# Seven-product quads whose sums are accumulated by TensorE on a copied bank, with a new plan of the work

## The chip, the cores and the metric

The kernel runs on one core of a Trainium2 chip. The metric is the device time of one execution in microseconds (us). PE is TensorE, DVE is VectorE, ACT is ScalarE, POOL is GpSimd, SP is SyncE. PE writes its products to PSUM, eight banks of 128 x 512 fp32, here the tiles bank0 to bank7; every engine but POOL works on them in this kernel.

## What is computed

Three parts follow each other: an attention, an expert with an ELU, and an expert with a gated SiLU behind an RMS norm.

```python
q_n, k_n = rmsnorm(q, g_q), rmsnorm(k, g_k)            # (4, 12, 448, 64)
scores = scale * np.matmul(q_n, k_n.transpose(0, 1, 3, 2))
attn = softmax(scores)                                  # row maximum taken off
x = np.matmul(attn, v).transpose(0, 2, 1, 3).reshape(1792, 768)

h = x @ w_in                                            # 768 -> 2048
g = np.where(h > 0, h, np.exp(np.minimum(h, 0)) - 1)
x = g @ w_out                                           # 2048 -> 768

xn = x / np.sqrt(np.mean(x * x, -1, keepdims=True) + 1e-6) * rms_g
g = xn @ w_gate                                         # 768 -> 1536
out = (g / (1 + np.exp(-g)) * (xn @ w_val)) @ w_out     # 1536 -> 768
```

The accuracy of fp32 is kept: each operand of a product is split into a rounded high part and the rest, and a product takes three matmuls (high by high, high by low, low by high).

## The kernel before

**Tiles.** Activations lie transposed, 128 features by the 448 tokens of one batch, so a matmul is 128 x 128 weights by 128 x 448 activations. `mm3` (L1329) issues the three matmuls of one split pair, as one step. `product` (L1343) sums several of them into a bank for the plain products.

**Stages.** `STAGES` (L718) has five: the first expert for batch 0, for batch 1, the second expert for batches 0 and 1, the first for 2 and 3, the second for 2 and 3. The attention is woven into the first ones. By `PLAIN` (L719) the first two stages and one group of the third use plain products; everything after that, from about 590 us on, is made of quads.

**Quads.** Two batches and two halves of the features make 2 x 2 blocks, and `quad` (L1363) forms the product of two such block matrices with seven block products in place of eight (Strassen's scheme in Winograd's form): `A11`, `A12`, `A22` are weight blocks and `S1` to `S4` sums of weight blocks, made beforehand; `B11`, `B21`, `B22` are activation blocks and `T1` to `T4` sums of them, which `combo` (L1390) makes. `part` (L1349) takes the next bank of the ring `r_m` and sums the two or three blocks of one product into it. There are 40 quads: 20 for gate and value of the second expert (`gv_quad`, ten calls of two, three blocks a product), 8 for the hidden layer of the first (`h_quad`, three blocks) and 12 for outputs (two blocks). The first product is copied to SBUF, and DVE adds up the others:

```python
copy(p1, part(w["A11"], tx["B11"]), "va")
p6 = part(w["S2"], tx["T2"]); tt(u2, p6, p1, ALU.add)
p2 = part(w["A12"], tx["B21"]); tt(p2, p2, p1, ALU.add); eat(0, 0, p2)
p7 = part(w["S3"], tx["T3"]); tt(u3, p7, u2, ALU.add)
```

`eat` is what uses a finished block (an activation function, a product with the gate, an addition to the output). `USE` (L753) is the order in which the weight blocks of a quad are loaded and taken in the last stage.

**Weights.** Raw weights come from HBM (`wr<-wst`, SP's queue), are split into high and low parts (`wc`, `wt`, `w`, `p`) by DVE, ACT and POOL while they are first used, and parts of them are stored to HBM (`pair<-w`, `kept<-wc`). In the last stage ready blocks are loaded by `b_ahead` (L806), which issues `w<-pair` on POOL's queue.

**The order of the work.** Nothing is issued directly. Every step is added to a `Plan` (L36) with its price on each engine that may run it; `tt`, `copy` and the like name the engines ("vag" is DVE, ACT or POOL), and a step with a PSUM operand can't go to POOL. `schedule` (L150) then lists the steps: `PASSES` forward and backward rounds from a random start (`SEED`), and after them the `MOVES`, each of which shakes the ranks of the steps planned between two times, and lists anew. `forward` (L216) takes the next step of the engine that is free first; where a step has a choice, the engine's own end plus a constant, `WAIT`, is compared with that of the others (L290). The constants are 2.5 for DVE, 0.3 for ACT and 0.4 for POOL. `issue` (L330) emits the steps in that order, so each engine runs its own in order, and fills empty places of PE before the first product with warm-up matmuls on the tile `small` (`IDLE`). All instructions are recorded at one line, L445, so tiles tell them apart. `phase` (L701) deals out the banks: three for `r_m` during the attention, six from phase 2, eight at the end.

## Time and profile before

| | us |
|---|---|
| timed runs | 1213.25, 1214.23, 1218.28 (median 1214.23) |
| profiled execution, first to last instruction (its span) | 1212.0 |
| PE busy | 1196.5 (99%) |
| DVE busy | 932.9 (77%) |
| ACT busy | 715.4 (59%) |
| POOL busy | 824.7 (68%) |

The page gives no time of its own for the profiled execution but its span; the timed runs lie above it. The engines work side by side, so their busy times don't add up to the span. In the rows further down, `out<-in` are tiles without their numbers, `xN` is how many instructions a row holds, and `[0.68 <-DVE pj]` says that the engine stood idle for 0.68 us and that DVE's step on the tile pj ended that.

### The profile page before, as it was taken

To read this page: it belongs to the slowest core of one execution; us is meant where nothing else is said; L and a number is where in the kernel's file an instruction comes from. 1 tells how busy PE (TensorE), PEld (TensorE's weight loads), DVE (VectorE), ACT (ScalarE), POOL (GpSimd) and SP (SyncE) were. 2 spreads that over 40 slices of the span, in tenths; PEclk is the share of its full clock that TensorE was granted. 3 is DMA by queue.
4 is the path that set the end of the run, shared out by engine and by line. 5 is a ranking of instruction groups with operands and counts; after the bars stand their busy time and mean duration, and the time that the engine had idled before them with its cause. 6 is when DMAs were issued, how large, how long until landed. Compare 5 with 4: busy or idle time off the path is not lost.

```text
span 1212.0 us, 18931 instructions
## 1 busy us (share of the span) xinstructions
PE 1196.5 (99%) x6262; PEld 1005.5 (83%) x6262; DVE 932.9 (77%) x1559; ACT 715.4 (59%) x1482; POOL 824.7 (68%) x686
## 2 busy tenths in 40 slices
PE   8999999999999999999999999999999999999998
PEld 7558777778777777777998999999999989999997
DVE  8788999889654579653498799957975799478687
ACT  6987878768666577655564465757653753222121
POOL 3678778788555485545887789857974878265362
PEclk9999999999999999999999999999999999999999
DMA  7678877878545598855499899696794855766766
GB/s 255 224 240 271 284 263 252 256 227 297 156 136 178 178 318 291 271 172 184 168 312 350 280 343 326 187 285 196 244 354 162 265 200 174 243 210 202 239 200 204
DMA packets 128294, 290.71 MB, mean 240 GB/s; under 512 B 16190, under 2 KB 77380, under 8 KB 128196
## 3 DMA queue, kind: packets, MB, share of 16 engines
q1 hardware_dynamic: 107028, 221.52, 53.7%
q0 software_dynamic: 12528, 58.99, 15.4%
q10 hardware_dynamic: 8640, 8.99, 2.9%
q8 instruction: 49, 0.80, 0.3%
q14 instruction: 49, 0.40, 0.1%
HBM read 193.34 MB, written 96.11 MB: 239 GB/s over the span
## 4 chain that ended last, share of the span: by engine, by line
PE 87%; DVE 5%; ACT 4%; issue 2%; DMA 1%; POOL 0%; ACTq 0%; DVEq 0%; POOLq 0%
PE bank L445 87%; DVE bank L445 1%; ACT tbig L445 1%; DMA w<-pair 1%; DVE wc L445 1%; ACT p L445 1%; DVE ss L445 1%; DVE late L445 1%; DMA pair<-late 1%; DVE last L445 0%; ACT pt L445 0%; DVE tbig L445 0%; DVE xs L445 0%; DMA tk<-tok 0%; DVE wt L445 0%
## 5 line engine op out<-in xcount | busy, mean ns | idle before, releaser
L445 PE MATMUL bank<-xs,w 128*128 128x448 f32 x1755 | 405.4, 370 | 0.8 <-ACT tbig L445 0.8
L445 PE MATMUL bank<-gbig,w 128*128 128x448 f32 x1675 | 377.3, 370 | 0.4 <-DMA w<-pair 0.4
L445 PEld LDWEIGHTS bank<-xs,w 128*128 128x128 f32 x1755 | 322.7, 188 | 33.1 <-issue 5.9
L445 PEld LDWEIGHTS bank<-gbig,w 128*128 128x128 f32 x1675 | 309.1, 188 | 32.6 <-issue 6.1
L445 POOL TENSOR_TENSOR w<-wc,w 128x768 fp32r<-128x768 f32 (+1 forms) x100 | 184.4, 1845 | 62.0 <-ACT w L445 57.8
L445 PE MATMUL bank<-late,w 128*128 128x448 f32 x740 | 185.8, 366 | 0.1
L445 DVE TENSOR_REDUCE bank<-bank 128x1 f32<-128x448 f32 x168 | 99.3, 624 | 65.2 <-PE bank L445 64.7
L445 PEld LDWEIGHTS bank<-late,w 128*128 128x128 f32 x740 | 138.8, 188 | 12.0 <-DVE late L445 0.4
L445 ACT ACTIVATE pt<-bank 128x384 f32<-128x384 f32 (+2 forms) x191 | 85.4, 459 | 43.5 <-PE bank L445 34.9
L445 ACT ACTIVATE p<-bank,nm,rr 128x448 f32<-128x448 f32 x126 | 90.0, 718 | 25.7 <-DVE nm L445 12.9
L445 DVE SCALAR_TENSOR_TENSOR wc<-wc,wt 128x768 int32<-128x768 int32 x68 | 92.4, 1360 | 14.5 <-ACT wc L445 8.7
L445 ACT ACTIVATE w<-wc 128x768 fp32r<-128x768 f32 (+1 forms) x80 | 62.6, 786 | 38.8 <-PE bank L445 33.2
L445 DVE TENSOR_TENSOR tbig<-bank,tbig 128x448 f32<-128x448 f32 x101 | 61.5, 618 | 18.1 <-PE bank L445 15.6
L445 DVE TENSOR_SCALAR wt<-wr 128x768 uint16<-128x768 uint16 x68 | 73.4, 1080 | 2.1 <-DMA wr<-wst 1.9
L445 POOL TENSOR_TENSOR w<-p,w 128x768 fp32r<-128x768 f32 (+1 forms) x33 | 62.1, 1886 | 18.5 <-ACT w L445 18.2
L445 PE MATMUL bank<-ident,p 128*128 128x128 f32 x441 | 71.2, 276 | 2.2 <-ACT pt L445 1.5
L445 POOL DMA_DIRECT2D w<-pair x60 | 33.5, 558 | 55.5 <-PE bank L445 54.4
L445 PEld LDWEIGHTS bank<-ident,p 128*128 128x128 f32 x441 | 53.5, 140 | 19.5 <-ACT pt L445 5.6
L445 ACT ACTIVATE tbig<-bank 128x448 f32<-128x448 f32 x69 | 37.1, 540 | 53.1 <-PE bank L445 45.9
L445 POOL TENSOR_SCALAR w<-wc 128x768 fp32r<-128x768 f32 (+1 forms) x39 | 33.3, 854 | 48.7 <-PE bank L445 45.6
L445 ACT ACTIVATE wt<-wr 128x768 uint16<-128x768 uint8 x46 | 50.1, 1088 | 11.8 <-DVE wc L445 10.6
L445 POOL TENSOR_TENSOR ql<-rw,qh 128x512 fp32r<-128x512 f32 x32 | 45.9, 1442 | 15.3 <-ACT qh L445 14.4
(247 smaller groups left out, 2199.5 us busy)
## 6 DMA issues: line engine op xcount, KB each, us to landing
wr<-wst SPq DMA_DIRECT2D x68, 768.0 KB
pair<-w SPq DMA_DIRECT2D x68, 384.0 KB
w<-pair POOLq DMA_DIRECT2D x33, 768.0 KB, 4.9
kept<-wc SPq DMA_DIRECT2D x52, 384.0 KB
wc<-kept SPq DMA_DIRECT2D x48, 384.0 KB
w<-pair POOLq DMA_DIRECT2D x24, 512.0 KB, 4.6
rw<-qk SPq DMA_DIRECT2D x21, 512.0 KB
tk<-tok SPq DMA_DIRECT2D x20, 480.0 KB
```

The source lines that it names most:

```text
L445: return lambda *a, **k: f(*[real(x) for x in a], **{n: real(x) for n, x in k.items()})
```

## The change

`quad` no longer copies the first product to SBUF. The product stays in its bank, a copy of it goes to a second bank `u`, and later products are accumulated by PE onto one or the other: `S2`, `S3` and `A22` onto `u`, `A12` onto the first product, `S4` onto that of `S1`. What `u` held after `S2` and after `S3` is copied to SBUF (`s2`, `s3`), and two additions remain. `part` gets the bank to add to, `mm3` and `block` pass that on, `USE` follows the new order, `combo` turns the sign of `T4`, and `phase` deals `r_m` its banks in another order. `Plan` gets other constants: more passes, another seed, `WAIT` of 0.6 for DVE (it was 2.5) and 1.2 for POOL (it was 0.4), 143 moves in place of 20, and a seventh number in a move which, where it is not negative, replaces POOL's constant for the time window of the move (in steps of 25 us).

```diff
-    PASSES = 11
-    SEED = 47
+    PASSES = 20
+    SEED = 12
     MOVES = (
-        (645977, 260.9, 275.9, 8.0, 1, 0),
...
+        (456330, 559.5, 659.5, 0.0, 1, 1, 3.0),
+        (918116, 941.4, 961.4, 8.0, 1, 0, -1.0),
...
-    WAIT = {"v": 2.5, "a": 0.3, "g": 0.4}
+    WAIT = {"v": 0.6, "a": 0.3, "g": 1.2}
...
+        self.bias = [self.WAIT["g"]] * 80
...
-        for seed, lo, hi, size, own, more in self.MOVES:
+        for seed, lo, hi, size, own, more, bias in self.MOVES:
+            if bias >= 0:
+                for k in range(len(self.bias)):
+                    if lo <= 25 * k < hi:
+                        self.bias[k] = bias
...
-                mine = t + alts[e][0] + self.WAIT[e]
-                other = min(max(free[o], t) + self.BACK * back[o] + alts[o][0] + self.WAIT[o] for o in alts if o != e)
+                wait = dict(self.WAIT, g=self.bias[min(79, int(t / 25))])
+                mine = t + alts[e][0] + wait[e]
+                other = min(max(free[o], t) + self.BACK * back[o] + alts[o][0] + wait[o] for o in alts if o != e)
...
-    def block(mms, price):
+    def block(mms, price, onto=False):
...
-                T.matmul(o, l, r, start=start, stop=stop)
+                T.matmul(o, l, r, start=start, stop=stop, skip_group_check=onto)
...
-            r_j.t, r_m.t = banks[0:2], banks[2:8]
+            r_j.t, r_m.t, r_m.k = banks[0:2], [banks[j] for j in (2, 4, 3, 5, 6, 7)], 0
...
-    USE = ("A11", "S2", "A12", "S3", "S1", "A22", "S4")
+    USE = ("A11", "S1", "S2", "A12", "S3", "A22", "S4")
...
-    def part(w, x):
-        o = r_m.next()[:, 0:S]
+    def part(w, x, o=None):
+        first = o is None
+        if first:
+            o = r_m.next()[:, 0:S]
         for k in range(len(w)):
-            mm3(o, w[k], x[k], k == 0, k == len(w) - 1)
+            mm3(o, w[k], x[k], first and k == 0, k == len(w) - 1, not first)
...
-        u2, u3, u4, u7 = (r_tp.next() for _ in range(4))
-        p1 = r_tp.next()
-        copy(p1, part(w["A11"], tx["B11"]), "va")
-        p6 = part(w["S2"], tx["T2"])
-        tt(u2, p6, p1, ALU.add)
-        p2 = part(w["A12"], tx["B21"])
-        tt(p2, p2, p1, ALU.add)
-        eat(0, 0, p2)
-        p7 = part(w["S3"], tx["T3"])
-        tt(u3, p7, u2, ALU.add)
+        s2, s3, u7 = (r_tp.next() for _ in range(3))
+        p1 = part(w["A11"], tx["B11"])
+        u = r_m.next()[:, 0:S]
+        copy(u, p1, "va")
         p5 = part(w["S1"], tx["T1"])
-        tt(u7, p5, u3, ALU.add)
-        tt(u4, p5, u2, ALU.add)
+        part(w["S2"], tx["T2"], u)
+        copy(s2, u, "va")
+        part(w["A12"], tx["B21"], p1)
+        eat(0, 0, p1)
+        part(w["S3"], tx["T3"], u)
+        copy(s3, u, "va")
+        tt(u7, p5, s3, ALU.add)
         eat(1, 1, u7)
-        p4 = part(w["A22"], tx["T4"])
-        tt(p4, u3, p4, ALU.subtract)
-        eat(1, 0, p4)
-        p3 = part(w["S4"], tx["B22"])
-        tt(p3, p3, u4, ALU.add)
-        eat(0, 1, p3)
+        part(w["A22"], tx["T4"], u)
+        eat(1, 0, u)
+        part(w["S4"], tx["B22"], p5)
+        tt(p5, p5, s2, ALU.add)
+        eat(0, 1, p5)
...
-        tt(t2, t2, b21, ALU.subtract)
+        tt(t2, b21, t2, ALU.subtract)
```

The next three places are taken from the order in which the two kernels issue their instructions (the recording line is L445 before and L566 after; a number behind a tile's name tells its buffer). The first is POOL at the head of the program, where q and k are split into qh and ql for the first products. Before:

```order
L445 TENSOR_TENSOR ql_103<-rw0_100,qh_102 128x512
L445 TENSOR_TENSOR rsb1_125<-rsb1_125 1x128
L445 TENSOR_TENSOR gbig_88<-wr1_92,gbig_88 128x512
L445 TENSOR_SCALAR qh_102<-rw0_100 128x512
L445 TENSOR_TENSOR ql_103<-rw0_100,qh_102 128x512
L445 TENSOR_TENSOR gbig_88<-wr1_92,gbig_88 128x512
L445 TENSOR_SCALAR qh_102<-rw0_100 128x512
L445 TENSOR_TENSOR ql_103<-rw0_100,qh_102 128x512
```

After:

```order
L566 TENSOR_TENSOR rsb1_125<-rsb1_125 1x128
L566 TENSOR_TENSOR gbig_88<-wr1_92,gbig_88 128x512
L566 TENSOR_SCALAR w0_95<-wc0_93 128x768
L566 TENSOR_SCALAR xs14_78<-xf0_126 128x448
L566 TENSOR_SCALAR wc0_93<-wr1_92 128x768
L566 TENSOR_TENSOR xs15_79<-xf0_126,xs14_78 128x448
L566 TENSOR_TENSOR ql_103<-rw0_100,qh_102 128x512
L566 TENSOR_SCALAR wc0_93<-wr0_91 128x768
L566 TENSOR_TENSOR gbig_88<-tbig_90,gbig_88 128x448
```

Four of the eight steps on qh and ql before are followed by one in the nine rows after; the others run on DVE and ACT, and steps on weights (wc, w) and activations (xs) have taken their places on POOL.

DVE at the first gate quads, about 636 us in the trace of before; wc, wt, wr and w are weights on their way to the split parts, tbig and pt the sums of the quads. Before:

```order
L445 TENSOR_TENSOR tbig_90<-bank5_132,tbig_90 128x448
L445 TENSOR_TENSOR bank6_133<-bank6_133,tbig_90 128x448
L445 TENSOR_TENSOR tbig_90<-bank7_134,tbig_90 128x448
L445 SCALAR_TENSOR_TENSOR pt0_107<-pt0_107,bank6_133 128x448
L445 TENSOR_TENSOR tbig_90<-bank2_129,tbig_90 128x448
L445 SCALAR_TENSOR_TENSOR wc0_93<-wc0_93,wt0_94 128x768
L445 TENSOR_TENSOR bank4_131<-bank4_131,tbig_90 128x448
L445 TENSOR_TENSOR tbig_90<-bank2_129,tbig_90 128x448
L445 TENSOR_SCALAR wt0_94<-wr0_91 128x768
L445 TENSOR_TENSOR bank3_130<-tbig_90,bank3_130 128x448
L445 SCALAR_TENSOR_TENSOR pt0_107<-pt0_107,tbig_90 128x448
L445 SCALAR_TENSOR_TENSOR pj0_109<-pj0_109,bank4_131 128x448
```

After:

```order
L566 COPY bank6_133<-bank5_132 128x448
L566 SCALAR_TENSOR_TENSOR wc0_93<-wc0_93,wt0_94 128x768
L566 TENSOR_TENSOR late9_5603<-xf0_126,late9_5603 128x448
L566 TENSOR_SCALAR wt0_94<-wr1_92 128x768
L566 SCALAR_TENSOR_TENSOR wc0_93<-wc0_93,wt0_94 128x768
L566 CAST w0_95<-wc0_93 128x768
L566 TENSOR_TENSOR bank5_132<-pt0_107,bank5_132 128x448
L566 TENSOR_TENSOR w0_95<-wc0_93,w0_95 128x768
L566 TENSOR_TENSOR gbig_88<-bank5_132,gbig_88 128x448
```

The runs of additions between banks and tbig are gone; a copy from bank5 to bank6 stands there, and steps on the weights (`CAST w0`, `TENSOR_TENSOR w0`) and activations (late) stand closer together.

PE at the end of the program, the last quad; before, bank6 holds the product of S3, bank7 of S1, bank2 of A22 and bank0 of S4. Before:

```order
L445 MATMUL bank6_133<-gbig_88,w2_97 128x448 x3
L445 MATMUL bank7_134<-late11_6829,w3_98 128x448
L445 MATMUL bank7_134<-late14_9414,w3_98 128x448
L445 MATMUL bank7_134<-late11_6829,w3_98 128x448
L445 MATMUL bank7_134<-late15_9436,w3_98 128x448
L445 MATMUL bank7_134<-gbig_88,w3_98 128x448
L445 MATMUL bank7_134<-late15_9436,w3_98 128x448
L445 MATMUL bank2_129<-gbig_88,w3_98 128x448 x3
L445 MATMUL bank2_129<-late11_6829,w3_98 128x448
L445 MATMUL bank2_129<-late12_9390,w3_98 128x448
L445 MATMUL bank2_129<-late11_6829,w3_98 128x448
L445 MATMUL bank0_127<-late14_9414,w0_95 128x448
```

After, where bank3 is `u` (S3, then A22) and bank5 gets S4:

```order
L566 MATMUL bank3_130<-late13_9327,w3_98 128x448
L566 MATMUL bank3_130<-gbig_88,w3_98 128x448
L566 MATMUL bank3_130<-late13_9327,w3_98 128x448
L566 MATMUL bank3_130<-gbig_88,w3_98 128x448 x6
L566 MATMUL bank3_130<-late11_6802,w3_98 128x448
L566 MATMUL bank3_130<-late12_9304,w3_98 128x448
L566 MATMUL bank3_130<-late11_6802,w3_98 128x448
L566 MATMUL bank5_132<-late14_9334,w0_95 128x448
L566 MATMUL bank5_132<-gbig_88,w0_95 128x448
L566 MATMUL bank5_132<-late14_9334,w0_95 128x448
```

S1 no longer stands between S3 and A22, and both go to the same bank, with nothing between them; the copy of that bank to `s3` comes between the two on ACT.

## Rows read from the trace of the kernel before

**Rows 1.** The page: busy time of each engine, and PE's granted clock in slices.
```profile
PE 1196.5 (99%) x6262; PEld 1005.5 (83%) x6262; DVE 932.9 (77%) x1559; ACT 715.4 (59%) x1482; POOL 824.7 (68%) x686
...
PEclk9999999999999999999999999999999999999999
```

**Rows 2.** The table by stretches: length, busy us of each engine (instructions), clock, DMA.
```profile
0.00:16.75 16.75, 15.18 (x128) 14.26 (x128) 10.95 (x35) 8.56 (x9) 4.71 (x9) 1.00 0.74 275
16.75:100.00 83.25, 78.97 (x469) 47.03 (x468) 68.98 (x158) 69.99 (x178) 54.84 (x49) 1.00 0.73 242
100.00:250.00 150.00, 149.78 (x812) 116.19 (x811) 139.75 (x202) 120.54 (x249) 121.90 (x87) 1.00 0.78 263
250.00:590.00 340.00, 337.90 (x1848) 263.14 (x1847) 218.57 (x384) 225.01 (x501) 210.38 (x159) 1.00 0.65 216
590.00:1000.00 410.00, 407.79 (x1999) 374.59 (x1998) 337.87 (x531) 241.44 (x454) 321.57 (x257) 1.00 0.79 264
1000.00:1207.30 207.30, 206.85 (x1017) 190.28 (x1015) 155.10 (x253) 49.87 (x93) 111.29 (x129) 1.00 0.67 212
1207.30:1212.00 4.70, 0.00 (x0) 0.00 (x0) 1.64 (x3) 0.00 (x0) 0.00 (x0) 1.00 0.38 146
```

**Rows 3.** Timeline at 1199 us: start, us, engine, operation, instructions; matmuls and a copy.
```profile
1199.22 0.77 PE L445 MATMUL bank<-late,w 128*128 128x448 f32 x3
...
1199.83 0.97 PE L445 MATMUL bank<-gbig,w 128*128 128x448 f32 x4
1200.03 0.54 ACT L445 ACTIVATE tbig<-bank 128x448 f32<-128x448 f32 x1 [8.21 <-PE bank L445]
```

**Rows 4.** Groups of instructions by form: busy us, mean ns, idle time before.
```profile
L445 DVE TENSOR_TENSOR tbig<-bank,tbig 128x448 f32<-128x448 f32 x101 | 61.5, 618 | 18.1 <-PE bank L445 15.6 <-ACT tbig L445 1.6
L445 POOL DMA_DIRECT2D w<-pair x60 | 33.5, 558 | 55.5 <-PE bank L445 54.4 <-DVE bank L445 0.5
L445 PE MATMUL bank<-small 128*128 128x128 f32 x106 | 14.7, 299 | 1.0 <-DVE small L445 1.0
...
L445 DVE COPY pt<-bank 128x384 f32<-128x384 f32 x1 | 0.6, 558 | 0.4 <-PE bank L445 0.4
...
L445 DVE CAST xs<-xf 128x448 fp32r<-128x448 f32 x1 | 0.4, 385 | 0.0
```

**Rows 5.** Timeline from 632.9 to 639.2 us: DVE, POOL and PE's wait.
```profile
632.93 0.94 DVE L445 SCALAR_TENSOR_TENSOR wc<-wc,wt 128x768 int32<-128x768 int32 x1
...
635.39 0.62 DVE L445 TENSOR_SCALAR wt<-wr 128x768 uint16<-128x768 uint16 x1
...
635.81 1.86 POOL L445 TENSOR_TENSOR w<-p,w 128x768 fp32r<-128x768 f32 x1 [3.77 <-ACT w L445]
...
636.15 2.35 DVE L445 SCALAR_TENSOR_TENSOR wc<-wc,wt 128x768 int32<-128x768 int32 x1
...
639.08 0.47 PE L445 MATMUL bank<-qh,w 128*128 128x448 f32 x1 [0.68 <-DVE pj L445]
```

**Rows 6.** Timeline from 981.9 to 984.8 us: POOL, DVE and PE's wait.
```profile
981.93 1.17 POOL L445 TENSOR_TENSOR xs<-xf,xs 128x448 fp32r<-128x448 f32 x1
...
982.51 2.16 DVE L445 TENSOR_TENSOR late<-tbig,late 128x448 fp32r<-128x448 f32 x1
...
984.73 0.47 PE L445 MATMUL bank<-late,late 128*128 128x448 f32 x1 [1.53 <-DVE late L445]
```

**Rows 7.** Timeline of the end: a wait for weights, the last matmul, DVE.
```profile
1197.90 0.87 PE L445 MATMUL bank<-gbig,w 128*128 128x448 f32 x3 [0.36 <-DMA w<-pair]
...
1206.92 0.36 PE L445 MATMUL bank<-gbig,w 128*128 128x448 f32 x1
...
1207.69 0.62 DVE L445 TENSOR_TENSOR bank<-bank,xf 128x448 f32<-128x448 f32 x1
```

**Rows 8.** Groups of DVE by form, from 0 to 590 us.
```profile
L445 DVE SCALAR_TENSOR_TENSOR wc<-wc,wt 128x768 int32<-128x768 int32 x48 | 66.0, 1375 | 12.0 <-ACT wc L445 6.8 <-POOL wc L445 2.9
L445 DVE TENSOR_SCALAR wt<-wr 128x768 uint16<-128x768 uint16 x49 | 51.8, 1057 | 0.2
```

More of the change, by code (lines that the diff above doesn't have):

```diff
@@ L1326, in attention, with mm3 @@
                 yield from tail(i, u)
-    def mm3(o, w, x, first, last):
+    def mm3(o, w, x, first, last, onto=False):
         wh, wl = w
         xh, xl = x
-        block([(o, wh, xh, first, False), (o, wh, xl, False, False), (o, wl, xh, False, last)], 0.611)
+        block([(o, wh, xh, first, False), (o, wh, xl, False, False), (o, wl, xh, False, last)], 0.611, onto)
     gs = {}
```

152 lines of the change are left out of this document (133 added, 19 removed).

## The prediction

> **What bounds the kernel now.** I read the page's engine lines first. PE is busy 1196.5 us of a span of 1212.0, and its granted clock stands in the top tenth in all 40 slices, so all of it runs at the higher of the clock's two levels, 2.4 GHz [rows 1]. A busy PE need not be a PE at its peak, so the second view is the table by stretches. From 590 to 1000 us PE starts 1999 matmuls in 410 us, and from 1000 to 1207.3 us 1017 in 207.3: 0.204 to 0.205 us each, which is the pace of a row of three whose next row follows 0.61 us later [rows 2, 3]. There PE has nothing to give but its idle time. The same table gives that, as the stretch less the busy share: 1.57 us before 16.75 (the first products of q and k), 4.28 up to 100, 0.22 up to 250, 2.10 up to 590, 2.21 up to 1000, 0.45 up to 1207.3, and 4.70 us of a tail without a matmul. The sum is 15.5 us. That is the stake: the change leaves PE its 280 products of sub-blocks, so what it can gain lies inside these 15.5 us and the 14.7 us of warm-up matmuls on the tile small [rows 4], and what it can lose has no such limit.
>
> The third view is the timeline at the places where PE stands still. Two of them tell the same story. At 635.81 POOL starts an addition of 1.86 us after 3.77 idle ones; at 636.15 DVE starts the int32 operation on wc that took 0.94 us at 632.93, and now it takes 2.35; the step behind it on DVE, on pj, comes late, and PE waits 0.68 us [rows 5]. At 982.51 DVE's subtraction into late takes 2.16 us beside POOL's work, and PE waits 1.53 us [rows 6].
>
> **Unchanged work.** The order has 5984 matmuls on PE before and 5978 now (some of them the trace lists as two); the six fewer are warm-ups, 14.7/106 = 0.139 us each [rows 4], and I take **-0.8 us** (0 to -0.8) for them, since a warm-up stands where the plan expects an empty PE. DMAs are the same in number.
>
> **The quads.** Each of the 40 quads had 7 additions on DVE and one copy on ACT. It now has 2 additions and 3 copies, 116 of the 120 copies on ACT. DVE loses 200 x 0.618 = 124 us [rows 4], ACT gains 76 x 0.54 = 41 us [rows 3]. A copy from PSUM to PSUM on ACT stands in no row; the nearest is the copy from PSUM to SBUF of the same size, 0.54 us, and DVE's addition, 0.618, is the upper end; I take 0.54, the same engine. None of this is on the path by itself. What comes onto it are waits of PE: a product that adds onto a bank must wait until the copy has read or filled that bank, and every matmul behind it on PE waits with it. The cost of one such loop is read near the end of the trace: three matmuls start at 1199.22, the next four 0.61 later, the copy starts at 1200.03 and takes 0.54 [rows 3], and a waiting PE starts 0.06 us after its releaser (984.73, after 982.51 + 2.16 = 984.67 [rows 6]). So the loop is 0.20 + 0.54 + 0.06 = 0.80 us. In the order I counted the matmuls on PE between the one the copy waits for and the one that waits for the copy: 6 in 52 of the 120 cases, 3 in two, 0 in one, 8 or more in the rest. Six matmuls are 1.22 us and cover 0.80 with 0.42 to spare. Three cover 0.61 and leave 0.19 each. The one with nothing is the last quad's A22 behind S3 and costs 0.80. Together **+1.2 us**. The 52 lose only if ACT is in the middle of something: a copy of this shape that has just begun leaves 0.54 - 0.42 = 0.12 us. At worst that is 52 x 0.12 = 6.2 us. ACT is busy 291 of 617 us there (241.44 + 49.87 [rows 2]), 332 with the new copies, about half the time, and only a copy that began in the last fifth of its 0.54 hurts, so I take a tenth of the worst, **+0.6 us**. S4 waits longer, for the copy of S3's sum and then for DVE's u7, 0.80 + 0.20 + 0.618 + 0.06 = 1.68 us in all, but at least A22's six matmuls and what covers A22 lie between: 2.44 us.
>
> In the tail, the last matmul starts at 1206.92, its slot ends 0.20 later, and its addition could start at 1207.32 by the lag of [rows 3], but starts at 1207.69, because DVE still works through the quad's other sums [rows 7]. The new quad leaves DVE fewer of them just there: **-0.4 us** (0 to -0.4).
>
> **The new plan.** POOL goes from 691 to 257 instructions, 87 of these DMA issues; DVE goes from 1561 to 1902, with 196 fewer in the quads and 537 more from POOL and ACT. The stalls of [rows 5] and [rows 6] are made by operations of DVE and POOL that hold each other up; with so few left on POOL I count both as gone: 0.68 + 1.53 = **-2.2 us** (0 to -2.2).
>
> The Trainium skill, in SBUF — State Buffer, under SBUF: two separate sides, has VectorE and GpSimd take the port pair that they share by an exclusive lock, for a whole instruction. By that rule a POOL operation that is no longer there gives DVE back its whole wait, and the sum would be as above; 2.35 against 0.94 us [rows 5] agrees.
>
> In the attention and the plain stages (16.75 to 590 us) PE idles 6.6 us [rows 2]. The order has 78 PE steps there with six or fewer instructions of cover before, and 48 now, so in proportion 6.6 x 30/78 = **-2.5 us** (-6.6 to +2: the stalls of the same kind in [rows 5, 6] are 0.68 and 1.53, and one more of each is 2). What speaks against it is DVE's load: 281 more DVE instructions stand before the first quad. Between a cast, 0.385 [rows 4], and a two-input operation of 768, 0.94 [rows 5], I take 0.55, near a copy of 384 from PSUM, 0.558 [rows 4], of the kind that moves there from ACT: +155 us. What comes back is the time lost beside POOL: the int32 step's mean is 1.375 us against 0.94 alone, the cast's of wt 1.057 against 0.62, so 48 x 0.435 + 49 x 0.437 = 42 us [rows 5, 8]. DVE, 438 us until 590 [rows 2], then has 438 + 155 - 42 = 551, 93%. It still fits under PE.
>
> **Sum.** 1212.0 - 0.8 + 1.2 + 0.6 - 0.4 - 2.2 - 2.5 = 1207.9 us of span. The three timed runs, 1213.25, 1214.23 and 1218.28 us, lie 1.25 to 6.3 above that profile's span, their median 2.2, so the forecast is 1207.9 + 2.2 = **1210.1 us**, a gain of 0.3%.
>
> **Rivals.** (1) Clearly faster. The head and the attention improve more than in proportion, because steps that took POOL 1.2 to 1.9 us [rows 5, 6] now take DVE half of that: stalls of 6.6 us fall to 1, and the 52 covers cost nothing. 1212.0 - 0.8 + 1.2 - 0.4 - 2.2 - 5.6 = 1204.2, with 2.2 that is 1206.4. For it: 30 fewer short covers. Against it: much of what PE waits for in the attention comes through ACT, which keeps its load.
>
> (2) Slower. DVE becomes the bound before 250 us. There it is busy 68.98 + 139.75 = 208.7 of 233.25 us [rows 2], so 24.5 are free. The stretch is two fifths of the time before the quads, so some 112 of the 281 instructions; priced at 0.94 they bring 105 us, against a return of at most 0.4 of POOL's 54.84 + 121.90 us there [rows 2], 71: 34 us more in 24.5 free, and the 9.5 over fall on PE. The point from which it decides is DVE at 100% from 100 to 250 us. With the other terms at their bad ends it gives 1212.0 + 9.5 + 1.2 - 0.4 + 2.2 = 1224.5. Against it: many of the moved steps are casts and copies of 0.385 to 0.558 us.
>
> (3) Weights late. The loads w<-pair are issued by POOL in 0.558 us [rows 4], and one of them stopped PE for 0.36 us before [rows 7]. Now 81 casts from SBUF to SBUF stand on DVE, one before. If each of ten issues in the last stage slips by a cast of 0.385, and PE waits for half of that, that is 1.9 us on the forecast, 1212.0 in all.
>
> The Trainium skill, in SBUF — State Buffer, on the "DVE blocks DMA" trap, says that such a cast keeps GpSimd from writing the descriptors of the DMAs it issues; no row before shows it, and by it this rival is the one that holds.
>
> (4) The change doesn't do what it says: adding onto a filled bank costs PE more than a first matmul. Rows of three, one first and two that add, show one pace for both [rows 3], so it would cost nothing, and the time is the forecast's.
>
> **How the numbers follow.** A difference of 0.5% (6.1 us) is about what a measurement of this kernel can tell from no change. The forecast with (3) and (4), all within that bound: 0.52. Rival 1: 0.38. Rival 2: 0.10. So faster 0.38, same 0.52, slower 0.10. The range leaves a tenth at each end: below, rival 1 with the last 1 us of its stalls, the rest of the tail's wait and a run at the lower edge (1.25 instead of 2.2), about 1203; above, the forecast with the 52 covers at their worst (+5.6) and part of the 2 us that the attention may lose, about 1217. Rival 2 lies outside.
>
> **What would show it.** Idle time of PE from 590 to 1207 us below 3 us, and none of it behind DVE's late or pj: the POOL term holds. Waits of PE for ACT's copies from bank to bank of over 2 us in sum: the covers' term is too small. DVE over 97% from 100 to 250 us and PE below 145 of 150: rival 2. PE waiting for w<-pair: rival 3. PE idle below 2 us from 16.75 to 100: rival 1.

## The result, and the profile after

| | before | after |
|---|---|---|
| timed runs, median (lowest to highest), us | 1214.15 (1213.25 to 1218.28) | 1224.94 (1222.53 to 1225.98) |
| profiled execution's own time, us | not given | 1224.75 |
| its span, us | 1212.0 | 1222.9 |
| DVE busy, us | 932.9 | 995.7 |
| ACT busy, us | 715.4 | 725.1 |
| POOL busy, us | 824.7 | 253.1 |

The change makes the kernel slower: ratio 1.0082, 95% interval 1.0063 to 1.0101. The forecast was 1210.1 us with a range up to 1217. The page of after, its engine line and its clock line, against [rows 1]:

```profile
PE 1203.9 (98%) x6250; PEld 1007.8 (82%) x6250; DVE 995.7 (81%) x1900; ACT 725.1 (59%) x1455; POOL 253.1 (21%) x252
...
PEclk9999999999999999999999999999999999999999
```

PE is busy 7.4 us longer with the same products, so part of the loss hides inside "busy". The clock line shows nothing, since a slice is some 30 us long and nine tenths and more read alike there. The table by stretches of after (length, then busy us of PE, PEld, DVE, ACT, POOL, then PE's granted clock, DMA share, GB/s), against [rows 2]:

```profile
0.00:16.75 16.75, 15.79 (x117) 14.81 (x117) 10.88 (x37) 8.97 (x10) 0.65 (x5) 1.00 0.74 277
16.75:100.00 83.25, 77.47 (x450) 44.28 (x447) 77.60 (x200) 73.29 (x169) 1.27 (x1) 0.96 0.69 223
100.00:250.00 150.00, 149.04 (x801) 117.61 (x800) 144.98 (x274) 120.79 (x230) 26.41 (x22) 1.00 0.78 263
250.00:590.00 340.00, 337.70 (x1846) 259.90 (x1845) 281.71 (x550) 209.92 (x451) 72.67 (x56) 1.00 0.66 218
590.00:1000.00 410.00, 405.99 (x1982) 372.22 (x1981) 346.71 (x621) 238.28 (x457) 109.76 (x95) 1.00 0.77 260
1000.00:1218.45 218.45, 217.79 (x1066) 198.98 (x1064) 132.58 (x222) 73.80 (x138) 42.30 (x73) 1.00 0.67 214
```

POOL does 1.27 us of work between 16.75 and 100 us, where it did 54.84. And there the granted clock is 0.96, not 1.00.

Where the time goes can't be read by laying the two tables side by side, since the later stretches hold other work. All versions issue the same 6156 matmuls besides warm-ups. So I gave each matmul the mean spacing that its shape has in the trace of before, added these up in the order of each trace, and took the moment at which a trace has done as much of the sum as the kernel before has at a mark. The difference is how far behind it is there; where shapes come in another order it can be off by some tenths. Executions that issue their first 350 us as the kernel before does (e1, e5, h1) stand 0.4 to 0.6 us behind it at the mark 100, so half a microsecond is noise. For the changed kernel, and for the runs that the next section tells of (us behind at the mark):

| mark in before | after | e5 | e7 | f1 | f2 | f3 | f4 | h2 |
|---|---|---|---|---|---|---|---|---|
| 100 | 3.96 | 0.41 | 1.74 | 0.48 | 2.93 | 3.97 | 4.60 | 1.35 |
| 350 | 7.59 | 0.49 | 4.31 | 0.28 | 7.63 | 14.38 | 14.69 | 1.87 |
| 590, first quad | 6.50 | -0.31 | 3.07 | 0.22 | 10.47 | 14.43 | 14.83 | 1.98 |
| 760 | 5.37 | -1.44 | 1.96 | -1.27 | 9.78 | 16.64 | 15.86 | 1.42 |
| 850 | 8.62 | 2.79 | 5.23 | -0.66 | 12.44 | 16.60 | 20.06 | 1.61 |
| 980 | 8.08 | 1.93 | 4.38 | 1.72 | 17.59 | 19.49 | 22.91 | 1.58 |
| 1000 | 9.94 | 2.35 | 4.74 | 2.59 | 15.72 | 21.66 | 23.28 | 0.87 |
| 1206 | 11.32 | 4.23 | 5.90 | 2.03 | 18.46 | 29.42 | 25.96 | 0.35 |

So the changed kernel loses 6.5 us before its first quad, gains 1.1 by 760, loses 3.2 up to 850, 1.9 about 990 and some more by the end. The tail gives 0.4 back: its last matmul starts 4.70 us before the end of the span, in the kernel before 5.08.

**Three places in the trace of after.** First, DVE and POOL, in the same columns, after and then before:

```profile
140.00:160.00 20.00, 19.98 (x112) 14.78 (x113) 20.00 (x41) 16.66 (x34) 0.00 (x0) 1.00 0.66 230
740.00:750.00 10.00, 10.00 (x50) 8.95 (x49) 10.00 (x21) 5.01 (x11) 0.00 (x0) 1.00 1.00 308
```

```profile
140.00:160.00 20.00, 20.00 (x112) 14.59 (x111) 19.45 (x29) 16.88 (x38) 16.01 (x13) 1.00 0.73 261
740.00:750.00 10.00, 10.00 (x51) 9.07 (x50) 9.95 (x16) 4.46 (x10) 10.00 (x8) 1.00 1.04 349
```

DVE is as full as a row can show, and POOL has not one instruction. Before, POOL ran beside a DVE that was nearly as full, but with fewer, longer steps (29 and 16 against 41 and 21).

Second, the timeline of after about 990 us (start, us, engine, operation, in brackets the idle time before and its releaser):

```profile
988.60 1.15 DVE L566 TENSOR_TENSOR xs<-last,xs 128x448 fp32r<-128x448 f32 x2
...
989.02 5.47 POOL L566 TENSOR_TENSOR xs<-last,xs 128x448 fp32r<-128x448 f32 x1
...
992.89 0.61 DVE L566 TENSOR_TENSOR xs<-last,xs 128x448 fp32r<-128x448 f32 x1
...
994.54 0.68 PE L566 MATMUL bank<-xs,w 128*128 128x448 f32 x2 [1.83 <-POOL xs L566]
```

A POOL step takes 5.47 us here; one of the same kind took 1.17 in [rows 6]. Between 988.07 and 993.50 DVE runs ten additions and subtractions with both inputs in SBUF, one right behind the other; POOL's step ends 0.99 us after the last of them. In [rows 5, 6] DVE had to wait for POOL; here POOL waits for a whole run of DVE steps, and PE for POOL.

Third, PE's granted clock, slices of 1 us in after, then the same slices in run e8, whose first 600 us are issued in the same way:

```profile
26.00:27.00 1.00, 0.55 (x3) 0.27 (x5) 1.00 (x4) 1.00 (x5) 0.00 (x0) 0.85 0.65 266
27.00:28.00 1.00, 1.00 (x5) 0.63 (x5) 1.00 (x5) 1.00 (x4) 0.00 (x0) 0.50 0.02 3
...
32.00:33.00 1.00, 1.00 (x7) 0.88 (x5) 1.00 (x4) 0.32 (x1) 0.00 (x0) 0.50 0.00 1
```

```profile
26.00:27.00 1.00, 0.69 (x5) 0.48 (x5) 1.00 (x5) 1.00 (x5) 0.00 (x0) 1.00 0.11 45
27.00:28.00 1.00, 1.00 (x8) 0.72 (x7) 1.00 (x2) 1.00 (x4) 0.00 (x0) 1.00 0.01 3
...
32.00:33.00 1.00, 1.00 (x7) 0.48 (x3) 1.00 (x4) 1.00 (x4) 0.00 (x0) 1.00 0.17 20
```

In after, the clock dips: it stands at the lower level, 1.2 GHz, from 26.7 to 33.5 us, after three waits between 22 and 27 us:

```profile
22.57 1.28 PE L566 MATMUL bank<-gbig 128*128 128x448 f32 x4 [0.74 <-ACT p L566]
24.50 0.87 PE L566 MATMUL bank<-gbig 64*128 64x448 f32 x5 [0.66 <-ACT p L566]
26.81 1.48 PE L566 MATMUL bank<-gbig 64*128 64x448 f32 x5 [0.45 <-ACT tbig L566]
```

In e8 the same steps, with waits of 0.72, 0.66 and 0.44 us, stay at 2.4 GHz. At the mark of 100 us after is 3.96 us behind, e8 1.73: by this pair the dip costs 2.2 us, and by run e4, which issues these steps alike, has a dip as long and is 3.05 behind, 1.3. The same happens once more behind the wait of 1.83 us above: from 996.1 to 999.5 us after runs at 1.2 GHz and loses 1.85 us between the marks 980 and 990, e8, with the same wait and no dip, 0.32. So a dip costs 1.5 us there.

A dip comes in some executions of the same steps and not in others, but not equally often in both plans: of the six traces whose first 36 us are issued as in after (after, e2, e4, e6, e7, e8), five have the first dip, 6.8 us long; of the five that start as the kernel before does (before, e1, e5, h1, h3), one has it, 3.4 us long.

### The profile page after: what moved, and what is told of

Its sections match the earlier page's. It is cut to its first block, busy times and chain, and to the rows that moved or that the text cites. A ratio compares the mean times of both kernels' runs of the same rounds, so it can differ in the third digit from the quotient of the medians.

```text
span 1222.9 us, 18564 instructions
## 1 busy us (share of the span) xinstructions
PE 1203.9 (98%) x6250; PEld 1007.8 (82%) x6250; DVE 995.7 (81%) x1900; ACT 725.1 (59%) x1455; POOL 253.1 (21%) x252
## 3 DMA queue, kind: packets, MB, share of 16 engines
q10 hardware_dynamic: 8640, 8.99, 2.7%
## 4 chain that ended last, share of the span: by engine, by line
PE 71%; DVE 18%; ACT 5%; issue 3%; DMA 1%; POOL 0%; ACTq 0%; SPq 0%; DVEq 0%
PE bank L566 71%; DVE bank L566 3%; DVE w L566 3%; DVE tbig L566 2%; DVE ybig L566 2%; DVE gbig L566 1%; DVE wc L566 1%; ACT tbig L566 1%; DVE pt L566 1%; ACT p L566 1%; DVE ss L566 1%; ACT pt L566 1%; DVE xs L566 1%; DVE wt L566 1%; DVE late L566 1%
## 5 line engine op out<-in xcount | busy, mean ns | idle before, releaser
L566 PE MATMUL bank<-xs,w 128*128 128x448 f32 x1746 | 404.5, 371 | 2.6 <-POOL xs L566 1.8
L566 PE MATMUL bank<-gbig,w 128*128 128x448 f32 x1674 | 379.9, 369 | 2.7 <-DVE pt L566 1.1
L566 PEld LDWEIGHTS bank<-xs,w 128*128 128x128 f32 x1746 | 320.6, 188 | 37.3 <-issue 8.0
L566 PEld LDWEIGHTS bank<-gbig,w 128*128 128x128 f32 x1674 | 309.2, 188 | 34.9 <-issue 4.5
L566 PE MATMUL bank<-late,w 128*128 128x448 f32 x750 | 187.5, 366 | 0.0
L566 PEld LDWEIGHTS bank<-late,w 128*128 128x128 f32 x750 | 140.7, 188 | 11.8
L566 ACT ACTIVATE p<-bank,nm,rr 128x448 f32<-128x448 f32 x126 | 90.6, 722 | 48.4 <-DVE nm L566 42.2
L566 DVE TENSOR_REDUCE bank<-bank 128x1 f32<-128x448 f32 x168 | 99.0, 622 | 16.0 <-PE bank L566 15.7
L566 DVE TENSOR_TENSOR w<-wc,w 128x768 fp32r<-128x768 f32 (+1 forms) x98 | 93.3, 954 | 6.0 <-ACT w L566 5.1
L566 ACT ACTIVATE tbig<-bank 128x448 f32<-128x448 f32 x90 | 48.8, 542 | 73.0 <-PE bank L566 72.3
L566 ACT ACTIVATE pt<-bank 128x384 f32<-128x384 f32 (+2 forms) x136 | 61.8, 464 | 26.5 <-PE bank L566 20.1
L566 DVE SCALAR_TENSOR_TENSOR wc<-wc,wt 128x768 int32<-128x768 int32 x68 | 69.6, 1024 | 6.1 <-ACT wc L566 4.2
L566 ACT ACTIVATE wt<-wr 128x768 uint16<-128x768 uint8 x57 | 61.9, 1086 | 19.8 <-DVE p L566 8.6
L566 PE MATMUL bank<-ident,p 128*128 128x128 f32 x441 | 71.2, 282 | 1.5 <-ACT pt L566 0.5
L566 ACT ACTIVATE w<-wc 128x768 fp32r<-128x768 f32 (+1 forms) x70 | 54.8, 782 | 27.2 <-PE bank L566 18.8
L566 PEld LDWEIGHTS bank<-ident,p 128*128 128x128 f32 x441 | 53.8, 143 | 19.3 <-issue 3.2
L566 POOL TENSOR_SCALAR w<-wc 128x768 fp32r<-128x768 f32 (+1 forms) x11 | 10.6, 968 | 266.1 <-DVE nm L566 161.5
L566 POOL DMA_DIRECT2D w<-pair x60 | 32.1, 536 | 135.8 <-PE bank L566 135.7
L566 ACT ACTIVATE wc<-wr 128x768 f32<-128x768 f32 x55 | 49.4, 905 | 12.8 <-DMA wr<-wst 5.4
L566 PE MATMUL bank<-pt,rv 128*64 128x448 f32 x252 | 53.1, 550 | 0.0
L566 POOL TENSOR_TENSOR w<-wc,w 128x768 fp32r<-128x768 f32 (+1 forms) x21 | 38.2, 1819 | 70.9 <-ACT w L566 62.9
L566 DVE TENSOR_TENSOR tbig<-bank,tbig 128x448 f32<-128x448 f32 x43 | 26.6, 619 | 32.0 <-ACT tbig L566 23.0
```

Source lines behind the costliest of these rows:

```text
L566: return lambda *a, **k: f(*[real(x) for x in a], **{n: real(x) for n, x in k.items()})
```

## The experiments

The medians of all runs that are told of here, against the kernel before in the same batch:

| run | what it is | median, us | ratio (95% interval) |
|---|---|---|---|
| e1 | plan of before up to the first quad, joined there | 1227.19 | 1.010 (1.008 to 1.012) |
| e2 | its mirror with old quads | 1239.08 | 1.0203 (1.0177 to 1.0228) |
| e3 | after, two casts from ACT to POOL | 1226.01 | 1.0091 (1.007 to 1.0112) |
| e4 | after, one step from POOL to DVE | 1223.01 | 1.0065 (1.0042 to 1.0087) |
| e5 | plan of before up to 350 us, rest of after | 1219.80 | 1.0049 (1.0034 to 1.0064) |
| e6 | plan of after up to 570 us, rest of before | 1220.33 | 1.0059 (1.0039 to 1.0079) |
| e7 | after, 68 steps back to POOL, 36 to 300 us | 1221.85 | 1.0065 (1.005 to 1.008) |
| e8 | after, 55 steps to POOL, 665 to 800 us | 1224.53 | 1.0087 (1.007 to 1.0104) |
| f1 | old quads, old constants, no moves | 1216.55 | 1.0023 (1.0013 to 1.0032) |
| f2 | new quads, old constants, no moves | 1230.59 | 1.0133 (1.0118 to 1.0148) |
| f3 | old quads, new constants, no moves | 1242.75 | 1.023 (1.021 to 1.0251) |
| f4 | new quads, new constants, no moves | 1240.55 | 1.0213 (1.0197 to 1.0228) |
| h1 | before, two collisions taken away | 1215.19 | 1.0014 (1.0005 to 1.0023) |
| h2 | before, 131 steps taken off POOL | 1215.76 | 1.0013 (1.0003 to 1.0023) |
| h3 | e5 and e4 in one | 1217.13 | 1.0026 (1.0015 to 1.0038) |

The theory was at first that the loss is made where the traces show it, by the new plan of the attention (theory A); the rival was that the quads' form and DVE's load cost the time and it only shows early. In the e and h runs `schedule` returns a list written out in the file, so that a step's engine or place can be changed and everything else stays. The first 3152 steps are the same in both kernels, which makes it possible to join one plan's beginning to the other's end. All diffs below stand for such a change of the list.

**Joined at the first quad (e1, e2).**

```diff
-        return order, best[2]
+        # steps 0 to 3151 in the other kernel's order and on its engines, the rest as here
+        return joined(other, here, 3152), engines
```

What was expected of e1:

> The first 3152 steps (attention and plain products, up to the first quad) take their engines and order from the plan of the kernel before, all quads and what stands behind them from the changed kernel's plan. Theory A (the loss sits where the two traces show it: 6.5 us of the 11 before the first quad, made by the new plan there): 1224.9 - 6.5 = 1218.4 us, within 1 us, and no dip of the granted clock before 100 us. Theory B (the new quads and DVE's load cost the time, and what the attention loses is only lost early instead of late): no change, 1223 to 1226 us.

What was expected of e2:

> The mirror: the old quads with their plan, behind an attention planned as in the changed kernel. Theory A: 1214.2 + 6.5 = 1220.7 us, within 1 us. Theory B: as the kernel before, 1213 to 1216 us.

Neither number came. In e1 the attention's loss was gone as theory A has it (0.8 us behind at the mark 590), but 6.8 us were lost right behind the joint, with this wait:

```profile
600.30 2.69 PE L801 MATMUL bank<-xs,w 128*128 128x448 f32 x9 [3.35 <-ACT bank L801]
```

Right behind it e1's clock stands at 1.2 GHz, from 601.6 to 608.4 us, so a part of the 6.8 us is the clock's; how they divide isn't shown. This is a row of e1, in the columns of the table by stretches:

```profile
602.00:608.00 6.00, 4.92 (x13) 3.35 (x13) 1.79 (x2) 2.74 (x5) 4.28 (x4) 0.50 0.34 128
```

e2 lost 19 us at its joint, and its clock is at 1.2 GHz from 618.5 to 632.1 us. That the plans hand over with different work unfinished, and that a joint at one step number leaves the queues out of tune, is argued and not shown. The two totals say nothing on the theories, so I joined inside the plain products.

**Joined elsewhere (e5, e6).**

```diff
+        # e5: what the kernel before plans before 350 us, as there; the rest as in after
+        # e6: what the changed kernel plans before 570 us, as there; the rest as in before
```

What was expected of e5:

> As the first hybrid, but joined inside the plain products: all steps that the kernel before plans before 350 us take their engines and order from its plan, all others those of the changed kernel. Theory A (7 us of the loss come from the plan of the attention, where DVE is full and POOL empty; the first hybrid lost 6.8 us again at its joint alone): the 7 us up to 350 are gone, what the changed kernel loses later stays, 1224.9 - 7 = 1218, within 1.5 us. Theory B (time lost early is only lost later otherwise): 1223 us or more.

What was expected of e6:

> The mirror: the old quads and the old plan, but all steps that the changed kernel plans before 570 us take their engines and order from its plan. Theory A: the attention brings its 6.5 us of loss, 1214.2 + 6.5 = 1220.7, within 1.5 us. Theory B: 1213 to 1216 us.

Theory A holds within a few tenths of its bounds: e5 is 5.1 us below the changed kernel (7 were expected; the change's own dips vary from run to run), and e6, with the old quads and the old plan from there on, lies 6.4 above the median of before in its batch, 1213.97. The new plan of the attention costs 5 to 6.4 us, with old quads behind it and with new ones.

**The head of the attention (e3).**

```diff
-        eng[97], eng[158] = "a", "a"    # gbig<-wr, qh<-rw
+        eng[97], eng[158] = "g", "g"
```

> The changed kernel, with two of its steps on ACT (the casts gbig<-wr at 19.59 us and qh<-rw at 23.12 us) moved to POOL, where the kernel before had them; all else in place. Theory A (these 1.25 us of ACT delay the p steps for which PE waits 0.74 + 0.66 + 0.45 us between 22 and 27 us, and the clock falls to half because of these waits): the waits shrink by about 1.2 us, the clock stays at 1.00 from 26 to 34 us, and the time falls by 2.5 to 3.5 us, to about 1222. Theory B (this stretch is bound by DVE and ACT together, and the time comes back as other waits before 100 us): 1224 to 1226 us.

The dip went as theory A says: the clock stays at 1.00 from 20 to 40 us, and at the mark 36 the run is 0.68 us ahead of the kernel before, where after is 1.68 behind. The waits did not go. The second and the third became short, but the first grew, and the sum is 1.74 us against 1.85:

```profile
22.21 1.24 PE L801 MATMUL bank<-gbig 128*128 128x448 f32 x4 [1.31 <-ACT p L801]
23.60 0.87 PE L801 MATMUL bank<-gbig 64*128 64x448 f32 x5 [0.16 <-ACT p L801]
25.91 0.87 PE L801 MATMUL bank<-gbig 64*128 64x448 f32 x5 [0.27 <-ACT tbig L801]
```

So nearly all that e3 has gained at the mark 36 is the dip: e8, with the waits of after and no dip, is 0.50 us ahead there. Then, at 104.67, PE waits 1.24 us for DVE, and by the marks 120 and 300 e3 is 2.83 and 6.40 us behind (after 3.41 and 6.96); the median is 1226.01, theory B's number. The time came back as other waits within 80 us. It need not have: e8, with the two casts on ACT, is 1.3 and 5.0 us behind at these marks and keeps what it gained. Why the moved casts make later steps late isn't shown.

**POOL's work given back (e7), or taken away from before (h2).**

```diff
+        for i in GIVEN:         # e7: 35 steps of DVE, 33 of ACT, all on POOL before
+            eng[i] = "g"
```

What was expected of e7:

> The changed kernel, in whose attention (36 to 300 us) 68 steps go back to POOL, which had them before: 35 of DVE, 33 of ACT; the order stays. Theory A (DVE and ACT are full there because POOL has nothing, and PE runs at DVE's pace): DVE's busy time from 100 to 250 us falls from 145 to about 130 us, and of the 5 us lost between 36 and 300 us at least half comes back: 1222 or less. Theory B (POOL's steps are slow and hold DVE up, so that the work is better off on DVE): 1225 or more.

What was expected of h2:

> The kernel before, in its order, with 131 of the 249 POOL steps of attention and plain products that the change takes off POOL moved as there (104 to DVE, 27 to ACT); the old quads stay. Theory A (taking work off POOL is what costs the attention its time): 2 to 4 us slower than the kernel before, lost between 36 and 350 us. Theory B (the order of the new plan costs it, the engine by itself nothing): 1213 to 1215.

The stretch from 100 to 250 us in e7, then in h2, columns as above:

```profile
100.00:250.00 150.00, 148.77 (x802) 117.33 (x800) 142.36 (x263) 109.77 (x215) 63.45 (x51) 1.00 0.79 265
```

```profile
100.00:250.00 150.00, 150.00 (x809) 116.27 (x809) 134.57 (x228) 127.70 (x259) 58.66 (x47) 1.00 0.78 265
```

e7 gains 3.1 us over after and is 3.1 us behind at the first quad instead of 6.5, so about half comes back, as A says, though DVE only falls from 145 to 142.4 and not to 130. Of the time given back to DVE and ACT, it was ACT's (120.8 to 109.8) that moved more. In h2 POOL is halved in the kernel before, and the attention loses 2.0 us up to 590; the median is 1.8 us higher with an interval of 0.4 to 2.8. That lies between the numbers of the two theories. So the steps taken off POOL make a part of the 6.5 us: 2.0 by h2, and 2.7 by e7, which is 0.9 us behind at the mark 36, before its first moved step, where after is 1.7. The dip at the head, which e7's trace has too (23.9 to 30.8 us), makes another 1.3 to 2.2. Some 1.6 to 3.2 us are left and may lie in the order of the list; that is a remainder, not something that a run showed by itself.

**DVE in the quads (e8).**

```diff
+        for i in QUADS:         # 55 steps of DVE between 665 and 800 us
+            eng[i] = "g"
```

> The changed kernel, in whose quads from about 665 to 800 us 55 steps of DVE go to POOL, which has not one step there; the order stays. Theory A (DVE is busy 10.0 of 10 us from 740 to 800 and the waits at 794, 803 and 782 us are its backlog): these waits, 2 us in sum, go down to below 0.7 us, and 1.5 to 2 us come back: 1223. Theory B (POOL holds DVE up): 1225 or more.

The wait that should have gone, in after and then in e8:

```profile
803.09 2.09 PE L566 MATMUL bank<-gbig,w 128*128 128x448 f32 x9 [1.08 <-DVE pt L566]
```

```profile
800.89 1.28 PE L801 MATMUL bank<-gbig,w 128*128 128x448 f32 x5 [1.22 <-DVE pt L801]
```

DVE fell to 8.99 of 10 us from 740 to 750, but this wait stayed, and what the shorter waits at 782 and 794 gave back was lost between 700 and 760. Theory A fails here: a full DVE is not what PE waits for at the end of the quads of the hidden layer. Just before this wait DVE itself stands idle for ACT, in after

```profile
800.65 0.63 DVE L566 SCALAR_TENSOR_TENSOR pt<-pt,tbig 128x448 f32<-128x448 f32 x1 [0.80 <-ACT pt L566]
...
802.41 0.62 DVE L566 SCALAR_TENSOR_TENSOR pt<-pt,bank 128x448 f32<-128x448 f32 x1 [0.33 <-ACT pt L566]
```

and in e8 for 1.18 and 0.33 us at the same two steps: steps on pt that go to and fro between ACT and DVE are what PE waits for. The median, 1224.53, lies between the numbers of the two theories. Between the marks 790 and 800 all versions with new quads lose (after 1.45 us, f2 1.95, f4 2.93), and those with old quads don't (f1 0.20, f3 0.00). So that loss goes with the form, in three lists each way (the third old one is the kernel before, the measure itself). An explanation, argued only: an old quad's products are independent and the planner may issue them in any order, while in a new one S2, S3 and A22 follow each other on one bank, so that where the quads end and the output products begin nothing is left to put between.

**The POOL step that waits for DVE (e4, h3).**

```diff
-        eng[5226] = "g"         # xs<-last,xs
+        eng[5226] = "v"
```

What was expected of e4:

> The changed kernel, with one step of POOL (xs<-last,xs at 989.02 us, 5.47 us long) moved to DVE. Theory A (POOL stands still beside a run of two-input DVE steps, PE waits 1.83 us for it and the clock falls to half for some 3.5 us, which costs another 1.6): the step takes 0.6 us, the clock stays at 1.00, and the time falls by 3.4 us to 1221.5, within 0.7. Theory B (DVE is full there, and PE waits for another of its steps instead): 1224 to 1226 us.

What was expected of h3:

> The hybrid whose first 350 us follow the plan of the kernel before, and the step xs<-last,xs on DVE, both in one. Theory A (the two losses are separate and add up): 1219.8 - 1.9 = 1217.9, within 1 us. Theory B (the second repair has its gain from time lost before): as the hybrid, 1219.8.

PE's wait is gone, and so is the dip behind it: between the marks 980 and 990 e4 is 1.78 us faster than the kernel before, where after is 1.85 slower. That is 3.6 us in the profiled executions. In the medians it is 1.9, so e4 ends between the numbers of the two theories. A dip that comes in some executions only would explain the difference, but no run shows which of the timed executions had it. h3 is 2.7 us below e5 and inside theory A's bounds, so the two repairs add up.

**Form and constants apart (f1 to f4).**

```diff
-    PASSES = 20
-    SEED = 12
+    PASSES = 11
+    SEED = 47
...
-    WAIT = {"v": 0.6, "a": 0.3, "g": 1.2}
+    WAIT = {"v": 2.5, "a": 0.3, "g": 0.4}
...
+    MOVES = ()
```

(That is f2, against after; f1 and f3 have the quads of before, f3 and f4 the constants of after, all four an empty `MOVES`.)

What was expected of f1:

> The kernel before with an empty MOVES: the plain list of the planner with its old constants (WAIT 2.5 for DVE, 0.4 for POOL). The base of a two by two: quads old or new, constants (PASSES, SEED, WAIT) old or new, none with moves. Both theories: some 3 to 8 us above the kernel before, 1217 to 1222, since the moves are gone.

What was expected of f2:

> New quads, old constants, no moves: 577 steps besides DMA issues stay on POOL or thereabouts. Theory A (the planner's new preference makes the loss, the quads' form costs 1 us of covers): within 2 us of the run with old quads and old constants. Theory B (the form makes it, by waits of PE for the copies): 5 us or more above that run, and waits of PE for ACT's bank<-bank copies of over 3 us.

What was expected of f3:

> Old quads, new constants, no moves. Theory A: 5 to 9 us above the run with old quads and old constants, lost before the first quad, with DVE over 95% busy from 100 to 250 us. Theory B: within 2 us of it.

What was expected of f4:

> New quads, new constants, no moves. Theory A: as old quads with new constants, within 2 us; so again 5 to 9 us above the base. Theory B: as new quads with old constants, within 2 us.

The new constants cost 26.2 us with the old quads and 10.0 with the new ones. The new quads cost 14.0 us under the old constants and gain 2.2 under the new. Of the numbers expected of f2, f3 and f4 only theory B's for f2 came. Theory A has the sign of the constants right, but it gave them 5 to 9 us with DVE over 95% busy from 100 to 250 us, and in f3 DVE is at 93%; its claim that the form costs about 1 us is wrong too: behind the mark 590 the form costs 8.0 - 1.8 = 6.2 us more than the old one under the same constants, and gains 15.0 - 11.1 = 3.9 under the new ones. Theory B's number for f2, 5 us or more, came without its sign: PE waits 2.0 us in sum for ACT's copies from bank to bank there, not over 3. f2 also warns: its first 3152 steps and its constants are f1's, and yet the list that the planner ends with is 10.5 us behind at the first quad. One draw of the planner can weigh as much as a constant. Each of the four is one draw, and `PASSES` and `SEED` change together with `WAIT`; no run changed `WAIT` alone or tried other seeds. So how much of the 26.2 and 10.0 us is the preference for DVE, and how much the draw, is open. f1 itself came 0.45 us below its range. And DVE's load is no measure by itself, as this stretch shows in f1, then in f3:

```profile
100.00:250.00 150.00, 149.79 (x812) 116.29 (x811) 139.49 (x202) 120.76 (x248) 121.78 (x88) 1.00 0.77 263
```

```profile
100.00:250.00 150.00, 146.91 (x789) 113.74 (x789) 139.73 (x257) 117.12 (x237) 58.94 (x44) 1.00 0.77 259
```

DVE is equally busy, and f3 loses 5.5 us more between the marks 100 and 250. The 143 moves bring the changed kernel from f4's 1240.55 to 1224.94; the 20 old ones bring 2.4.

**The two collisions by themselves (h1).**

```diff
+        eng[3348] = eng[5283] = eng[5285] = "v"   # w<-p,w; xs<-last,xs; xs<-xf,xs
+        # 3348 behind DVE's steps on pj and pt, the other two behind DVE's late
```

> The kernel before, with three of POOL's steps moved to DVE: w<-p,w at 635.81 us, put behind the two steps that follow there on DVE, and xs<-xf,xs at 981.93 and xs<-last,xs at 983.06, put behind DVE's late. It takes away the two collisions that the prediction read off, and nothing else. Theory A (the prediction's term holds by itself: DVE's wc takes 0.94 instead of 2.35 us and late 0.6 instead of 2.16, and PE's waits of 0.68 and 1.53 us go): 1.5 to 2.2 us faster than the kernel before, about 1212. Theory B (another step is late in their place): within 0.5 us of it.

The two DVE steps of [rows 5, 6], and what came instead:

```profile
636.55 0.96 DVE L690 SCALAR_TENSOR_TENSOR wc<-wc,wt 128x768 int32<-128x768 int32 x1
...
982.60 0.62 DVE L690 TENSOR_TENSOR late<-tbig,late 128x448 fp32r<-128x448 f32 x1
...
986.78 3.90 DVE L690 TENSOR_TENSOR xs<-last,xs 128x448 fp32r<-128x448 f32 x1
```

```profile
713.22 2.19 POOL L690 TENSOR_TENSOR w<-p,w 128x768 fp32r<-128x768 f32 x1
713.84 2.38 DVE L690 SCALAR_TENSOR_TENSOR wc<-wc,wt 128x768 int32<-128x768 int32 x1
...
716.81 2.69 PE L690 MATMUL bank<-xs,w 128*128 128x448 f32 x12 [1.34 <-DVE xf L690]
...
1032.62 0.67 PE L690 MATMUL bank<-late,w 128*128 128x448 f32 x2 [0.81 <-DVE late L690]
```

The steps take what they take alone, 0.96 and 0.62 us, and PE gains 0.93 us at each place. Then new collisions arise: DVE's wc takes 2.38 us beside POOL's w, and PE waits 1.34 us for the step xf behind it; DVE's xs, one of the moved steps, takes 3.90 us beside a run of POOL steps, which costs PE 0.23; and PE waits 0.81 us at 1032.62. The median is 1.2 us above the kernel before, so theory A fails; theory B's mechanism is what the trace shows, though its bound was 0.5.

No version is faster than the kernel before; the best with new quads is h3, 3.2 us above it.

## Why the prediction was wrong, by its steps

**The new plan, attention: this step failed.** It gave -2.5 us, in proportion to the count of short covers (78 to 48), and the measured term is +6.5 up to the first quad. The count says how many PE steps stand close behind what they wait for. It doesn't say whether the engine that works for them gets there in time. What the runs showed in its place: the plan of the first 350 us alone is worth 5.1 us (e5), and with the old quads 6.4 (e6); the steps taken off POOL make 2.0 to 2.7 us of the term, the dip of the clock at the head 1.3 to 2.2, and the rest is open. In e3 two of three short waits nearly went, and what it had gained by the mark 36 was lost again within 80 us. The step on DVE's load didn't decide it either: it estimated 551 us of 590 and concluded "it still fits"; measured are 10.88 + 77.60 + 144.98 + 281.71 = 515.2, less than estimated, and time was lost all the same. That DVE is full in stretches (20.00 of 20 at 140 us) isn't shown to be the reason: f1 and f3 differ by 5.5 us with DVE equally busy, and e7 gains with DVE at 142.4 of 150.

**The new plan, collisions: wrong in sum.** The places of [rows 5] and [rows 6] did lose their waits: after gains 1.0 us between the marks 590 and 640. But the term was taken as -2.2 with nothing late next, and the same contention the other way round (5.47 us on POOL) gave 1.83 us of PE's wait back, and a dip of the clock behind it. h1 shows that even in the old kernel the two waits are not worth -2.2: the 0.93 us gained at each place are lost elsewhere. The sign that was set for this term, PE idle below 3 us from 590 us on and none of it behind DVE's late or pj, came by half: late and pj are gone, and PE idles 4.01 + 0.66 = 4.7 us up to its last matmul.
The Trainium skill, in SBUF — State Buffer, under SBUF: two separate sides, has the one that comes second block for the other's instruction; the trace agrees for one step against one (2.35 against 0.94 us), and shows more than one instruction's wait where a run of DVE steps stands on the other side.

**Covers and copies: right.** The bank-to-bank copies on ACT take 0.53 us (0.54 were taken):

```profile
L566 ACT ACTIVATE bank<-bank 128x448 f32<-128x448 f32 x38 | 20.1, 530 | 36.5 <-PE bank L566 36.4
```

The place without cover is the last quad, as forecast, with its three matmuls, the copy, and A22:

```profile
1214.48 0.78 PE L566 MATMUL bank<-gbig,w 128*128 128x448 f32 x3
...
1215.30 0.55 ACT L566 ACTIVATE tbig<-bank 128x448 f32<-128x448 f32 x1 [1.93 <-PE bank L566]
...
1215.90 0.88 PE L566 MATMUL bank<-gbig,w 128*128 128x448 f32 x3 [0.63 <-ACT tbig L566]
```

The slot of the last of the three ends at 1214.48 + 0.61 = 1215.09, and A22 starts 0.81 later: the loop of 0.80. Else PE waits for a bank copy once, 0.4 us. Together 1.2, against 1.2 + 0.6.

**Where the form costs, the prediction had no term**: 3.2 us between 760 and 850, of which 1.45 where the hidden layer's quads end. The steps looked at waits for copies alone. That the products lose the freedom to be issued in any order is the explanation argued above, not shown.

**The clock: no term.** The prediction took it as 1.00 throughout, by a line of tenths in which a dip of a few us doesn't show; for the trace of before it is so, by the 1.00 of every stretch in [rows 2]. Measured against e8, the dips of after make 2.2 + 1.5 = 3.7 us of the 10.9 in the profiled executions. They lie inside the losses at the head and about 990 us named above and don't add to them.

**Warm-ups and tail.** The six warm-ups saved nothing that the trace can show: at the mark 16.75 after is 0.16 us behind, where executions that start as before does differ from it by up to 0.7. The tail's -0.4 is measured as 5.08 - 4.70 = 0.38.

**Rivals.** Rival 1, clearly faster, fails with the same step: its sign was PE idle below 2 us from 16.75 to 100, and PE idles 83.25 - 77.47 = 5.78 there. Rival 2's time, 1224.5, is nearly the measured one, but by luck, by another sum: its sign was that DVE is at 100% from 100 to 250 us and PE loses 9.5 there; DVE is at 144.98 of 150, PE loses 1.9 between the marks 100 and 250. Rival 3 has no trace, though a sentence of the prediction has it as the one that holds: no wait of PE for w<-pair stands in after, and POOL issues these loads in 536 ns (558 before). Rival 4 neither: between the marks 640 and 740, where all is quads, PE keeps its spacing to within 0.2 us in sum. That slower had a tenth rests on the failed step: a preference that empties one of the three helpers was priced by mean durations, and e7 and h2 show that the emptied engine by itself costs 2 us and more.

**Open** is what in the new list costs the remaining 1.6 to 3.2 us of the attention's loss, how much of the constants' effect is one draw of the planner, and why the clock dips in one execution and not in the next.

## What to carry to other kernels

When an edit changes a planner's preference, the count of near waits and the mean load of an engine don't price it: here the same constants with another draw moved 10 us, and with one engine at equal load 5.5 us were lost. Where products are accumulated on one bank they are also put in a row; look at the places where a stage ends and the next one needs all its results, not only at the copies between them. Two engines that hold each other up can't be repaired one place at a time: taking two collisions away made others.

## What the hardware showed that I had not expected

- POOL stood for 5.47 us at one subtraction while DVE ran ten steps with both inputs in SBUF, and ended 0.99 us behind the last; the same in the other direction took DVE 3.90 us in h1.
- The same steps ran with the clock at 2.4 GHz throughout 20 to 40 us in one trace (e8), and at 1.2 GHz for 6.8 us in another (after), behind waits of PE of under 1 us each in both; the cost was 1.3 to 2.2 us.
- Adding onto a bank that ACT had filled didn't change PE's pace: from 1000 us on, 217.79 us for 1066 matmuls after and 206.85 for 1017 before, 0.204 and 0.203 each. A copy from bank to bank takes 0.53 us on ACT and 0.63 on DVE.
